# Loading the first batch's q and k in runs of eight rows per partition instead of four

## The chip, the cores and the metric

The kernel runs on one core of one Trainium2 chip. The metric is the device time of one execution in microseconds. Every kernel is run several times, beside the kernel before on the same chip. In the profile lines PE is TensorE, DVE VectorE, ACT ScalarE and POOL GpSimd. SBUF is the on-chip memory that the tiles stand in, PSUM the one that TensorE's results stand in.

## The reference

```python
def _attn_ref(q, k, v, tau):                      # B, N, C = 4, 6016, 256
    qn = q / (np.linalg.norm(q, axis=1, keepdims=True) + 1e-06)
    kn = k / (np.linalg.norm(k, axis=1, keepdims=True) + 1e-06)
    s = kn.transpose(0, 2, 1) @ qn / tau
    s = s - s.max(-1, keepdims=True)
    a = np.exp(s)
    a /= a.sum(-1, keepdims=True) + 1e-09
    return v @ a

def _moe_ref(x, w_gate, w_val, w_out):            # x: the 24064 x 256 rows of the above
    gate = 1.0 / (1.0 + np.exp(-(x @ w_gate)))
    return (gate * (x @ w_val)) @ w_out           # d_ff = 1536
```

The norms run over the 6016 rows, so one batch's scores, norms and 256 x 256 attention matrix need all of that batch's q and k before anything can be done with v. For batches 1 to 3 this is hidden behind the feed-forward of the batch before. For batch 0 nothing hides it.

## The kernel before

A partition holds 47 consecutive rows of a batch. Groups are four rows per partition (0 to 10), then two rows (group 11), then one (group 12). Group 0 comes as fp32 over two other queues; all else is loaded and cast to bf16 by DMAs that GpSimd issues, in one queue, in this order: q and k of groups 1 to 12, the first v, the expert weights (gate and value, in three column parts), the second v, the output weights.

```python
    def load_qk(b, t0, nt):
        tiles = []
        for name, src in (("q", q), ("k", k)):
            tl = qkpool.tile([P, TPC, C], BF16, tag=name, name=name + "_sb")
            nc.gpsimd.dma_start(out=tl[:, :nt, :], in_=rows(src, b)[:, t0 : t0 + nt, :])
            tiles.append(tl)
        qk[b, t0] = tiles
```

The work on batch 0, group by group: VectorE squares q, ScalarE squares k, VectorE adds both squares to bf16 accumulators, and TensorE adds the group to the scores. Small filler matmuls (`busy`) are meant to keep TensorE's clock up towards the end.

```python
    for g, (t0, nt) in enumerate(groups0):
        engines = (nc.vector, nc.scalar) if g < last0 else (nc.scalar, nc.vector)
        sq = [squares(0, t0, nt, w, engines[w], acc[w] if g == 0 else None) for w in range(2)]
        while adds:
            w, last_sq = adds.pop()
            nc.vector.tensor_tensor(out=acc[w], in0=acc[w], in1=last_sq, op=ALU.add)
        if 0 < g < n_acc:
            nc.vector.tensor_tensor(out=acc[0], in0=acc[0], in1=sq[0], op=ALU.add)
            if g < n_acc - 1:
                nc.vector.tensor_tensor(out=acc[1], in0=acc[1], in1=sq[1], op=ALU.add)
            else:
                adds.append((1, sq[1]))
        elif g:
            ends.append((sq, nt))
        if g == last0:
            norm_mms(ps_n0, acc, TPC, True, False)
            for n, (end, rows_n) in enumerate(ends):
                norm_mms(ps_n0, end, rows_n, False, n == len(ends) - 1, (1, 0) if n else (0, 1))
        for u in range(nt):
            score(0, t0, u)
        if n_acc - 4 <= g < n_acc:
            busy(1)
```

Then come the roots, the eps add (the 1e-6 of the reference is added to the norms) and the reciprocal, the scaled scores, the exponent, and the attention matrix folded into the expert weights (`ps_gh`); from there on TensorE runs to the end.

```python
    def norms_sqrt(b):
        s = st[b]
        s["r"] = attp.tile([P, 2 * CB], FP32, tag="r", name="r")
        nc.scalar.activation(out=s["r"], in_=s["n"], func=ACT.Sqrt)

    def norms_inv(b):
        r = st[b]["r"]
        nc.vector.tensor_scalar(out=r, in0=r, scalar1=1e-6, scalar2=None, op0=ALU.add)
        nc.vector.reciprocal(r, r)
```

## Time and profile before

| | before |
|---|---|
| time, median | 829.5 us |
| TensorE busy | 97% of the span |
| start to the first folded weight matmul (ps_gh) | 36.55 us |
| from there to the end | 791 us, TensorE without a break of note |
| DMA, 8 to 28 us | never idle, 209 GB/s written as bf16 |

The chain of waits reads from top to bottom as what had to end for the next piece to start. Its first 36 us are DMA, the rest is TensorE; so the kernel is bound by the bytes of batch 0 first and by TensorE afterwards, and only the first part can be touched by a change of loads. The prediction shows the lines.

### The profile page before, as it was taken

To read this page: it belongs to the slowest core of one execution; us is meant where nothing else is said; L and a number is where in the kernel's file an instruction comes from. 1 tells how busy PE (TensorE), PEld (TensorE's weight loads), DVE (VectorE), ACT (ScalarE), POOL (GpSimd) and SP (SyncE) were. 2 spreads that over 40 slices of the span, in tenths; PEclk is the share of its full clock that TensorE was granted. 3 is DMA by queue.
4 is the path that set the end of the run, shared out by engine and by line. 5 is a ranking of instruction groups with operands and counts; after the bars stand their busy time and mean duration, and the time that the engine had idled before them with its cause. 6 is when DMAs were issued, how large, how long until landed. Compare 5 with 4: busy or idle time off the path is not lost.

```text
span 827.7 us, 13626 instructions
## 1 busy us (share of the span) xinstructions
PE 806.9 (97%) x5122; PEld 498.5 (60%) x5134; DVE 591.5 (71%) x1027; ACT 390.8 (47%) x642; POOL 83.1 (10%) x159
## 2 busy tenths in 40 slices
PE   4799999999999999999999999999999999999998
PEld 2456666665665666665575666666566566666666
DVE  6777877787667777778767777777766666666665
ACT  4554444446644444445654444444655444444442
POOL 5532100002210100000311010000000000000000
PEclk9899999999999999999999999999999999999999
DMA  9999623226746443223876452223322323322211
GB/s 210 206 201 216 110 52 90 60 53 136 158 88 119 96 89 61 54 52 85 158 138 124 80 107 60 51 63 75 64 61 63 73 52 85 60 58 69 47 36 71
DMA packets 79026, 77.17 MB, mean 93 GB/s; under 512 B 50800, under 2 KB 55920, under 8 KB 78960
## 3 DMA queue, kind: packets, MB, share of 16 engines
q0 software_dynamic: 23920, 38.81, 28.1%
q1 hardware_dynamic: 54752, 36.91, 17.4%
q8 instruction: 40, 0.66, 0.3%
q10 hardware_dynamic: 288, 0.59, 0.2%
q14 instruction: 26, 0.21, 0.1%
HBM read 78.64 MB, written 24.64 MB: 125 GB/s over the span
## 4 chain that ended last, share of the span: by engine, by line
PE 94%; DMA 4%; DVE 1%; issue 0%; ACT 0%; POOL 0%; POOLq 0%
PE ps_o L88 30%; PE ps_gate L88 29%; PE ps_val L88 29%; PE ps_s L88 4%; DMA k_sb<-in_k_dram 3%; PE ps_gh L88 2%; DMA w_gate<-in_moe_w_gate_dram 1%; DVE hT L426 0%; ACT g_sb L425 0%; PE ps_end L88 0%; DVE sq L176 0%; PE ps_n L88 0%; POOL q_sb L97 0%; PE ps_tp L396 0%; DVE end L467 0%
## 5 line engine op out<-in xcount | busy, mean ns | idle before, releaser
L426 DVE TENSOR_TENSOR hT<-ps_val,g_sb 128x512 bf16<-128x512 f32 (+1 forms) x576 | 390.8, 679 | 205.6 <-ACT g_sb L425 201.0
L425 ACT ACTIVATE g_sb<-ps_gate 128x512 bf16<-128x512 f32 (+1 forms) x576 | 338.2, 588 | 386.2 <-PE ps_gate L88 380.2
L88 PE MATMUL ps_val<-vT,gh_H 128*128 128x512 bf16 (+1 forms) x1152 | 337.6, 375 | 0.3
L88 PE MATMUL ps_gate<-vT,gh_G 128*128 128x512 bf16 (+1 forms) x1152 | 337.5, 375 | 0.2
L88 PE MATMUL ps_o<-w_out_sb,hT 128*128 128x256 bf16 x2244 | 324.9, 273 | 0.0
L88 PEld LDWEIGHTS <-hT 128*128 128x128 bf16 x2268 | 221.0, 98 | 124.6
L88 PEld LDWEIGHTS <-gh_H 128*128 128x128 bf16 x1152 | 112.7, 98 | 132.1 <-issue 1.4
L88 PEld LDWEIGHTS <-gh_G 128*128 128x128 bf16 x1152 | 112.4, 98 | 37.6 <-ACT gh_G L379 0.2
L106 POOL DMA_DIRECT2D v_sb<-in_v_dram x48 | 25.5, 531 | 620.2 <-DMA vT<-v_sb 480.4
L452 DVE COPY out_sb<-ps_o 128x256 f32<-128x256 f32 x187 | 77.2, 413 | 12.6 <-PE ps_o L88 12.6
L88 PE MATMUL ps_s<-k_sb,q_sb 128*128 128x256 bf16 x376 | 70.5, 289 | 15.8 <-DMA k_sb<-in_k_dram 8.8
L88 PEld LDWEIGHTS <-q_sb 128*128 128x128 bf16 x376 | 38.6, 103 | 24.6 <-issue 9.6
L215 DVE TENSOR_TENSOR acc<-acc,sq 128x1024 bf16<-128x1024 bf16 (+1 forms) x66 | 44.1, 669 | 0.0
L176 DVE TENSOR_TENSOR sq<-q_sb 128x1024 bf16<-128x1024 bf16 (+2 forms) x44 | 29.3, 667 | 0.0
L97 POOL DMA_DIRECT2D q_sb<-in_q_dram x48 | 26.5, 552 | 15.2 <-DMA q_sb<-in_q_dram 7.3
L97 POOL DMA_DIRECT2D k_sb<-in_k_dram x48 | 26.2, 545 | 16.1 <-DMA k_sb<-in_k_dram 6.6
L176 DVE TENSOR_TENSOR sq<-k_sb 128x1024 bf16<-128x1024 bf16 (+2 forms) x34 | 22.4, 658 | 0.2 <-DMA k_sb<-in_k_dram 0.2
L174 ACT ACTIVATE sq<-k_sb 128x1024 bf16<-128x1024 bf16 (+1 forms) x11 | 11.2, 1019 | 13.6 <-DMA k_sb<-in_k_dram 13.6
L88 PE MATMUL ps_gh<-w_val,e_sb 128*128 128x512 bf16 x45 | 13.5, 379 | 0.2
L88 PEld LDWEIGHTS <-e_sb 128*128 128x128 bf16 x112 | 10.2, 98 | 5.3 <-DMA w_gate<-in_moe_w_gate_dram 0.6
L88 PE MATMUL ps_gh<-w_gate,e_sb 128*128 128x512 bf16 x41 | 12.7, 379 | 0.7 <-DMA w_gate<-in_moe_w_gate_dram 0.5
L425 ACT ACT_TABLE_LOAD x6 | 7.7, 1283 | 9.0 <-PE ps_gate L88 9.0
(69 smaller groups left out, 121.1 us busy)
## 6 DMA issues: line engine op xcount, KB each, us to landing
out_dram<-out_sb SPq DMA_DIRECT2D x44, 512.0 KB, 2.9
v_sb<-in_v_dram POOLq DMA_DIRECT2D x44, 256.0 KB, 3.8
q_sb<-in_q_dram POOLq DMA_DIRECT2D x43, 256.0 KB, 7.4
k_sb<-in_k_dram POOLq DMA_DIRECT2D x43, 256.0 KB, 8.1
out_dram<-out_sb SPq DMA_DIRECT2D x3, 384.0 KB, 3.1
w_gate<-in_moe_w_gate_dram POOLq DMA_DIRECT2D x3, 256.0 KB, 8.0
w_val<-in_moe_w_val_dram POOLq DMA_DIRECT2D x3, 256.0 KB, 8.1
w_out_sb<-in_moe_w_out_dram POOLq DMA_DIRECT2D x1, 768.0 KB, 13.3
```

The source lines that it names most:

```text
L88: nc.tensor.matmul(out, lhsT=lhsT, rhs=rhs, start=start, stop=stop, **kw)
L97: nc.gpsimd.dma_start(out=tl[:, :nt, :], in_=rows(src, b)[:, t0 : t0 + nt, :])
L106: nc.gpsimd.dma_start(out=v_sb[:, :nt, :], in_=rows(v, b)[:, t0 : t0 + nt, :])
L174: nc.scalar.activation(out=sq[:, :nt, :], in_=src[:, :nt, :], func=ACT.Square)
L176: engine.tensor_tensor(out=sq[:, :nt, :], in0=src[:, :nt, :], in1=src[:, :nt, :], op=ALU.mult)
L215: nc.vector.tensor_tensor(out=acc[:, :nt, :], in0=acc[:, :nt, :], in1=st[b]["sq", w][:, :nt, :], op=ALU.add)
L425: nc.scalar.activation(out=g_sb[:, :n], in_=ps_gate[:, :n], func=ACT.Sigmoid)
L426: nc.vector.tensor_tensor(out=hts[b, ci][:, f, :n], in0=ps_val[:, :n], in1=g_sb[:, :n], op=ALU.mult)
L452: nc.vector.tensor_copy(out=out_sb[:, s, :], in_=ps)
```

## The change

The intent: fewer and longer runs per partition for batch 0, so that the DMA queue has less overhead per byte. Groups 1 to 8 are loaded two at a time (eight rows, 8 KB read and 4 KB written per partition); groups 9 to 12 and all later batches keep their sizes. To hold eight rows the buffers are twice as large and there are 8 of them, not 12.

```diff
-    qkpool = pool("qkpool", NCH)
+    qkpool = pool("qkpool", 8)
...
-            tl = qkpool.tile([P, TPC, C], BF16, tag=name, name=name + "_sb")
+            tl = qkpool.tile([P, 2 * TPC, C], BF16, tag=name, name=name + "_sb")
             nc.gpsimd.dma_start(out=tl[:, :nt, :], in_=rows(src, b)[:, t0 : t0 + nt, :])
             tiles.append(tl)
-        qk[b, t0] = tiles
+        for u in range(0, nt, TPC):
+            qk[b, t0 + u] = [tl[:, u : u + TPC, :] for tl in tiles]
...
-    load_qk(0, *groups0[1])
+    pairs = [(t, 2 * TPC) for t in range(TPC, head - 3 * TPC, 2 * TPC)]
+    loads0 = pairs + [(t, n) for t, n in groups0 if t >= pairs[-1][0] + 2 * TPC]
+    load_qk(0, *loads0[0])
...
-    for t0, nt in groups0[2:]:
+    for t0, nt in loads0[1:]:
         load_qk(0, t0, nt)
```

## The prediction

> **What bounds the kernel now.** I read the page first (engine shares, the forty slices), then the chain of work that ended last from the start to 62 us, then the DMA rate between 9 and 27 us, and last the timeline between 22 and 38 us, engine by engine. The page says where to look:
>
> ```profile
> PE 94%; DMA 4%; DVE 1%; issue 0%; ACT 0%; POOL 0%; POOLq 0%
> ```
>
> From about 37 us to the end TensorE is the chain, and nothing in this change touches its instructions. The 4% of DMA is the only part that a different load of q and k can shorten. The chain in order of time shows it as one block at the head:
>
> ```profile
> 1.89 6.29 DMA k_sb<-in_k_dram
> ...
> 8.46 9.74 DMA k_sb<-in_k_dram
> ...
> 18.48 9.74 DMA k_sb<-in_k_dram
> ...
> 28.51 8.00 DMA w_gate<-in_moe_w_gate_dram
> ...
> 36.55 0.60 PE ps_gh L88 x2
> ```
>
> The columns are start, length and what. The loads of the first batch are back to back, and behind them in the same queue the first expert weights land at 36.51 us; TensorE starts the folded weights (ps_gh) then. This is a stretch set by bytes, not by latency: an issue is 9.74 us ahead of its landing only because about eight loads of 1.25 us each are queued. The DMA queue between 9 and 27 us:
>
> ```profile
> DMA packets 2066, 3.77 MB, mean 209 GB/s; under 512 B 227, under 2 KB 227, under 8 KB 2066
> q0 software_dynamic: 2066, 3.77, 112.1%
> ```
>
> 209 GB/s is of the bf16 written; twice that, 418 GB/s, is read as fp32. The engines are never idle here. The 2066 packets are 1839 data packets (2 KB written, 4 KB read) and 227 completion writes, so a run of four rows is one packet.
>
> Now the race at the end of the stretch, in the timeline (start, length, engine, line, operation, and the idle time before it with its releaser):
>
> ```profile
> 25.78 1.06 ACT L174 ACTIVATE sq<-k_sb 128x1024 bf16<-128x1024 bf16 x1 [1.43 <-DMA k_sb<-in_k_dram]
> 26.87 0.69 DVE L493 TENSOR_TENSOR acc<-acc,sq 128x1024 bf16<-128x1024 bf16 x1 [0.47 <-ACT sq L174]
> 27.48 0.68 DVE L176 TENSOR_TENSOR sq<-q_sb 128x1024 bf16<-128x1024 bf16 x1
> 28.20 0.69 DVE L491 TENSOR_TENSOR acc<-acc,sq 128x1024 bf16<-128x1024 bf16 x1
> 28.31 1.06 ACT L174 ACTIVATE sq<-k_sb 128x1024 bf16<-128x1024 bf16 x1 [1.47 <-DMA k_sb<-in_k_dram]
> 29.40 0.69 DVE L493 TENSOR_TENSOR acc<-acc,sq 128x1024 bf16<-128x1024 bf16 x1 [0.51 <-ACT sq L174]
> ...
> 31.88 0.69 DVE L489 TENSOR_TENSOR acc<-acc,sq 128x1024 bf16<-128x1024 bf16 x1
> ...
> 32.73 0.29 DVE L176 TENSOR_TENSOR sq<-k_sb 128x256 bf16<-128x256 bf16 x1 [0.16 <-DMA k_sb<-in_k_dram]
> ...
> 35.85 0.20 PE L88 MATMUL ps_r<-ones_bf,e_sb 128*128 128x1 bf16 x2 [0.35 <-ACT e_sb L316]
> ...
> 36.55 0.60 PE L88 MATMUL ps_gh<-w_gate,e_sb 128*128 128x512 bf16 x2 [0.49 <-DMA w_gate<-in_moe_w_gate_dram]
> ```
>
> Three things are to be seen. ScalarE starts a k square as each load lands, every 2.5 us. VectorE does three steps per group (square of q, add of q, add of k), spaced 0.61, 0.72 and 0.67 us when nothing holds it: 2.0 us in every 2.5, so it has 0.5 us of rest per group. And TensorE reached ps_gh 0.49 us before the weight landed, so the softmax branch (norms, exponent) has only half a microsecond of slack against the weight branch.
>
> **What the Trainium skill says.**
> 1. "DMA: Bandwidth & Descriptors", section "Where 436 GB/s comes from": the fabric gives 435 GB/s. The trace agrees that little is left: 418 GB/s, 96% of it. At the ceiling 1.049 MB (q and k of four rows) would take an estimated 2.41 us, not 2.51.
> 2. The same page, "Why small descriptors are slow (HBM only)": a fixed overhead of about 3 cycles per packet beside one cycle per 32 bytes. Estimate from it: 4096 bytes read are 128 + 3 cycles, 8192 are 256 + 3, so 1.2% less time per byte. No trace here has an 8 KB packet yet.
> 3. The same page, "Queues, rings and completion order": an engine alternates between its queues at packet granularity. Longer packets in the software queue can thus take share from the two fp32 loads of the first group, which ride another queue and took 4.8 and 5.0 us to land.
> 4. "TensorE: Matmul & The Clock Gate", "What's actually happening": an idle window of about 3.4 us brings half clock, a busy one brings it back. The trace agrees in kind: the same eight score matmuls took 1.03 us at 15.71 and 1.86 us at 18.24, after bursts with 1.5 us of idle.
>
> **The change, part by part.**
> - Removed: the first batch's groups 1 to 8 (rows 4 to 35) were 16 loads; they become 8 loads of twice the size. That is 8 x 128 = 1024 data packets and 8 x 16 = 128 completions fewer; the software queue should fall from 23,920 packets to 22,768, if a run of eight rows stays one packet. Bytes are the same.
> - DMA gain. 16 loads take 8 x 2.51 = 20.1 us. By the skill's 1.2%: 0.23 us. If the whole gap to 435 GB/s (0.10 us per pair of loads) is per packet and halves: 8 x 0.05 = 0.40 us. I take 0.3 us, on the landing of the last eight-row load and of everything behind it, the weights too (36.5 to about 36.2).
> - POOL issue: 8 issues of 0.53 us fewer; none was on the path, as POOL waited about 0.7 us for queue room before each. Worth 0.
> - Granularity, the cost. Group 7 (rows 28 to 31) used to land at 23.27; now it lands with group 8 at 25.76 (less the 0.3). VectorE therefore stands at 26.87 with the k add of group 7, where before it was at the k add of group 8: it is one group, 2.0 us, behind, and from there it has no rest. Walk it with the spacings above: k add 7 at 26.87; square, add, add of 8 at 27.48, 28.20, 28.87; of 9 at 29.48, 30.20, 30.87; square and add of q of 10 at 31.48 and 32.20; the two-row square at 32.87; the last k add at 33.36 instead of 31.88; the one-row square after 33.95 instead of 32.73. ScalarE is never late here (two squares of 1.06 us from 25.78, group 9 at 28.31). The norm matmuls end at about 34.6 instead of 33.35, 1.27 us later.
> - On the path: of the 1.27 us the first 0.49 are slack, so 0.78 remains. With the DMA gain both branches move 0.3 earlier, and the softmax branch is now the later one: 0.78 - 0.3 = +0.48 us.
> - Buffers: 8 of eight rows in place of 12 of four. Later batches take one per four-row group, a group every 8 slots of the schedule, loaded 20 slots ahead and used for about 8: four to five live at once. Eight are enough; worth 0. The one load of the first batch that reuses a buffer waits for group 0, whose last use is near 10 us.
> - After the start: about 790 us of TensorE chain, unchanged.
>
> Sum: 829.5 + 0.5 = 830.0 us.
>
> **The rivals.**
> (a) Long runs read better than the packet estimate, and VectorE catches up sooner. For it: someone chose to leave the last three groups short, which is what one does to keep the tail of the landing fine. Against: only 4% is left to the ceiling, 0.8 us over 20 us. It would make 828.7 to 829.3.
> (b) An eight-row run is cut into two packets, or its cast goes slower. Then only the backlog is left: +0.8, 830.3; slower packets by 5% would add 1 us. Nothing in the profile shows a packet over 4 KB read.
> (c) TensorE's clock. Score work now comes in 16 matmuls every 5 us with nearly 3 us of idle, so more of it runs at half clock; but 16 slow ones take 3.7 us, below 5, and with the filler matmuls from 25.8 on it is busy nearly without a break, so it should be at full clock by 30. If it were slow in the folded weights, up to 1.7 us would be added: 831.7.
> (d) Eight buffers hold up later loads. It would show as POOL waiting and TensorE idling after 100 us; TensorE is at 9 tenths in every slice now. I give it 3%.
> (e) The first fp32 group lands up to 0.5 us later (point 3). VectorE has 0.5 us rest per group before group 7, so it is absorbed: 0.
>
> **Range and chances.** The terms are -0.2 to -0.8 (DMA) and 0 to +0.8 (backlog), with (c) as a tail upward. Predicted 829.9, a touch below the sum because (a) is likelier than (b); 8 in 10 between 828.7 and 831.2. Two per cent is 16.6 us, more than half of the whole stretch that is touched: faster 0.01, same 0.98, slower 0.01.
>
> **What would show it.** The rate between 9 and 25 us: 421 to 425 GB/s read (210.5 to 212.5 in the page's count); 1152 packets fewer. ScalarE's k squares in twos, 5 us apart. VectorE without idle from about 26.6 to 33.6, and the one-row square near 33.7, not 32.7. Before ps_gh no wait for the weight load any more, but a longer one of ps_r for the exponent. TensorE's ps_gh from about 37.0. It is wrong if VectorE rests again before the last group, if ps_gh starts before 36.3, or if the time after 40 us grows by itself.

## The result and the profile after

The changed kernel took 830.08 us (median of 6 runs, 829.94 to 830.38) against 829.50 us (829.35 to 829.66, 6 runs). The ratio is 1.0007, with a 95% interval of 0.9994 to 1.0020: the same within 2%. Run once more later, it took 830.36 us against 829.71 us (ratio 1.0011). The interval includes 1. Still, in both rounds the slowest run of the kernel before (829.66, then 829.76) is faster than the fastest of the changed one (829.94, then 830.25); what the half microsecond is made of is read from the traces below.

The page of the changed kernel, packets of the software queue and the chain by engine:

```profile
q0 software_dynamic: 22768, 38.81, 28.3%
...
PE 94%; DMA 2%; DVE 2%; POOL 1%; ACT 0%; issue 0%; POOLq 0%; ACTq 0%
```

The packets fell by exactly the 1152 predicted, so an eight-row run stayed one packet. DMA lost half of its share of the chain (4% to 2%); VectorE (1% to 2%) and GpSimd (0% to 1%, its issues at the very start) took it over. The queue between 9 and 25 us of the changed kernel:

```profile
DMA packets 963, 3.40 MB, mean 212 GB/s; under 512 B 112, under 2 KB 112, under 8 KB 963
```

In the same window the kernel before moved 209 GB/s. Now the chain in order of time of the changed kernel (start, length, what), first 45 us:

```profile
6.26 18.92 DMA k_sb<-in_k_dram
...
25.26 1.07 ACT sq L180
26.35 0.69 DVE acc L499
27.05 0.61 DVE sq L182
27.68 0.69 DVE acc L497
...
32.57 0.61 DVE acc L495
...
33.23 0.67 PE ps_n L88 x20
...
34.12 0.74 DVE r L288
...
37.12 0.45 PE ps_gh L88 x2
```

Before, the chain went from loads to the weight load and into ps_gh. Now it leaves the DMA at 25.22 us, when the fourth eight-row k has landed, and goes through VectorE without a gap to the norms at 33 us. That is the backlog the prediction described. (The chain shows ps_gh at 37.12 us, where the ps_r matmuls before it end; it started at 36.98.) One line is odd: the eps add on `r`, four numbers per partition, lasts 0.74 us. The timeline around it, all engines, changed kernel:

```profile
33.09 0.28 DVE L182 TENSOR_TENSOR sq<-k_sb 128x256 bf16<-128x256 bf16 x1
...
33.80 1.06 POOL L150 DMA_DIRECT2D w_out_sb<-in_moe_w_out_dram  x1
...
34.12 0.73 DVE L288 TENSOR_SCALAR r<-r 128x4 f32<-128x4 f32 x1 [0.75 <-ACT r L284]
...
36.92 0.20 PE L88 MATMUL ps_r<-ones_bf,e_sb 128*128 128x1 bf16 x2 [0.36 <-ACT e_sb L322]
36.98 0.59 PE L88 MATMUL ps_gh<-w_gate,e_sb 128*128 128x512 bf16 x2
```

The same two lines of the kernel before:

```profile
33.08 0.73 POOL L139 DMA_DIRECT2D w_val<-in_moe_w_val_dram  x1
...
33.59 0.21 DVE L282 TENSOR_SCALAR r<-r 128x4 f32<-128x4 f32 x1 [0.56 <-ACT r L278]
```

In both kernels the eps add ends within 0.01 us of the end of a DMA issue on GpSimd (34.12 + 0.73 = 34.85 against 33.80 + 1.06 = 34.86; 33.59 + 0.21 = 33.80 against 33.08 + 0.73 = 33.81). Before, it started near the end of an issue; now it starts early in the long issue of the output weights. The Trainium skill, "SBUF — State Buffer", section "Who interferes with whom", offers a reason: VectorE and GpSimd share one pair of SBUF ports, `tensor_scalar` can enter a mode that needs both pairs, and whichever of the two starts first holds the pair for its whole instruction. Two of the experiments test this.

Everything after the start is moved as one block. Before, the second set of v transposes on TensorE starts at 50.04 us and the last matmul group (ps_end) at 822.96; after, at 50.47 and 823.39. Both differences are 0.43 us, which is also the difference of ps_gh (36.98 - 36.55). The medians differ by more, 0.58 us: the trace of the kernel before is of a run at 829.76 us, 0.26 above its median, and that of the changed kernel of one at 830.02, near its own.

### The profile page after: what moved, and what is told of

Same layout as the page of the kernel before. It is cut to its first block, busy times and chain, and to the rows that moved or that the text cites. A ratio compares the mean times of both kernels' runs of the same rounds, so it can differ in the third digit from the quotient of the medians.

```text
span 828.1 us, 13627 instructions
## 1 busy us (share of the span) xinstructions
PE 808.6 (98%) x5134; PEld 498.9 (60%) x5134; DVE 591.7 (71%) x1027; ACT 390.4 (47%) x642; POOL 78.8 (10%) x151
## 4 chain that ended last, share of the span: by engine, by line
PE 94%; DMA 2%; DVE 2%; POOL 1%; ACT 0%; issue 0%; POOLq 0%; ACTq 0%
PE ps_o L88 30%; PE ps_val L88 29%; PE ps_gate L88 29%; PE ps_s L88 4%; PE ps_gh L88 2%; DMA k_sb<-in_k_dram 2%; DVE sq L182 0%; DVE hT L432 0%; POOL q_sb L98 0%; DVE acc L497 0%; DVE acc L499 0%; ACT g_sb L431 0%; PE ps_n L88 0%; POOL k_sb L98 0%; PE ps_end L88 0%
## 5 line engine op out<-in xcount | busy, mean ns | idle before, releaser
L98 POOL DMA_DIRECT2D q_sb<-in_q_dram x44 | 24.1, 548 | 40.5 <-PE ps_s L88 14.6
L98 POOL DMA_DIRECT2D k_sb<-in_k_dram x44 | 24.0, 545 | 14.0 <-DMA k_sb<-in_k_dram 7.7
```

## The experiments

**Theory.** Three terms act in the first 37 us, and what they sum to is carried unchanged to the end: the longer runs bring the data earlier; the fourth eight-row load leaves VectorE a group behind with no rest left to catch up; and the eps add then falls into GpSimd's issue of the output weights. **Rivals:** the smaller pool of larger buffers costs the time; long runs cost time wherever they stand; the long eps add is something else than a port held by GpSimd.

All of these results were correct, and all times are medians of five runs (nine of the kernel before, in the same rounds).

### Buffers alone

```diff
-    loads0 = pairs + [...]                 # four-row loads, buffers as in the change
+    loads0 = groups0[1:]
```

> Eight buffers of eight rows as in the change, but every load four rows, as before. Theory (the change acts only in the first 37 us, by fewer and longer runs and by later group 7): 829.5 us like the kernel before, within 0.15; 23,920 packets in the software queue, score groups 2.51 us apart, folded weights (ps_gh) from about 36.5 us with a wait on the weight load. Rival (the smaller pool of larger buffers costs the time, by later loads or by addresses): 830.0 us, with ps_gh still at 36.5 and the time lost after 40 us.

829.40 us against 829.49 (ratio 0.9999, interval 0.9987 to 1.0012). ps_gh started at 36.27 us behind the weight load, and the time from the second transposes to ps_end was 772.92 us, as in the kernel before. The buffers cost nothing that shows; that rival falls. The loads are those of the kernel before, so the 0.28 us between the two traces at ps_gh is the spread from run to run: the first weights landed at 36.2 us here, at 36.5 there.

### The eps add reads PSUM

```diff
-        nc.scalar.activation(out=s["r"], in_=s["n"], func=ACT.Sqrt)
+        nc.scalar.activation(out=s["n"], in_=s["n"], func=ACT.Sqrt)
...
-        nc.vector.tensor_scalar(out=r, in0=r, scalar1=1e-6, ...)
+        nc.vector.tensor_scalar(out=r, in0=st[b]["n"], scalar1=1e-6, ...)
```

> The changed kernel, but the square roots of the norms stay in PSUM and VectorE's eps add reads them there, so that it has no SBUF source. Theory (the eps add took 0.73 us in the changed kernel because GpSimd held the shared SBUF ports while it wrote the descriptors of the output weight load): it takes 0.15 to 0.25 us, ps_gh starts about 0.5 us sooner, at 36.4 to 36.5, and the time is 829.5 us. Rival (the 0.73 us is something else, such as a late semaphore, or nothing that is on the path): the eps add or the step after it stays long and the time is 830.0 us.

829.63 us against 829.49 (ratio 1.0002, interval 0.9990 to 1.0015). The timeline of this kernel:

```profile
33.96 1.06 POOL L150 DMA_DIRECT2D w_out_sb<-in_moe_w_out_dram  x1
34.26 0.16 DVE L288 TENSOR_SCALAR r<-ps_n 128x4 f32<-128x4 f32 x1 [0.74 <-ACT ps_n L284]
34.46 0.18 DVE L289 RECIPROCAL r<-r 128x4 f32<-128x4 f32 x1
...
36.54 0.59 PE L88 MATMUL ps_gh<-w_gate,e_sb 128*128 128x512 bf16 x2
```

The same issue is under way and the add runs through it in 0.16 us. From the start of the add to ps_gh it now takes 2.28 us; in the changed kernel it was 2.86. So about 0.57 us of the add (0.73 - 0.16) was waiting. The reciprocal right after it reads and writes SBUF inside the same issue and takes 0.18 us, as in the kernel before: a source in SBUF alone does not make a VectorE instruction wait.

### The output weights are issued first

```diff
-    load_v(0, 1)
     nc.gpsimd.dma_start(out=w_out_sb, in_=moe_w_out.rearrange("(t p) c -> p t c", p=P))
+    load_v(0, 1)
```

> The changed kernel with GpSimd's issue of the output weight load (1.06 us) put ahead of the issue of the second v load (0.58 us). Theory (port lock): the output weight issue runs from about 33.3 to 34.3 us, the eps add can start at 34.1 and ends within 0.02 us of that issue's end, so it lasts about 0.2 us unless the v issue takes the port first, in which case it lasts until 34.85 again; ps_gh at about 36.45, 829.5 us. Rival (the 0.73 us belongs to VectorE or the semaphore, not to GpSimd): it stays 0.73 us whatever GpSimd does, 830.0 us.

830.15 us against 829.72 (ratio 1.0005, interval 0.9992 to 1.0017). The median did not fall to 829.5 as expected, and no run shows why; the trace is of the fastest of the five runs (829.80). In it the step under test did what the theory says:

```profile
33.51 1.05 POOL L149 DMA_DIRECT2D w_out_sb<-in_moe_w_out_dram  x1
34.37 0.20 DVE L288 TENSOR_SCALAR r<-r 128x4 f32<-128x4 f32 x1 [0.75 <-ACT r L284]
34.52 0.60 POOL L108 DMA_DIRECT2D v_sb<-in_v_dram  x1
...
36.68 0.59 PE L88 MATMUL ps_gh<-w_gate,e_sb 128*128 128x512 bf16 x2
```

The add starts later in the issue and ends again with it (34.57 against 34.56), so it lasts only 0.20 us. It ends with the issue in two other runs too, where it came early in it: 0.73 us with one end at 35.15 and the issue's at 35.16 (last pair only, below), and 0.64 us with 35.00 and 35.01 (three pairs, below). With the run above this settles that GpSimd's issue sets the end of this add when its source lies in SBUF. That the ports are the reason is the skill's explanation; the PSUM run and the reciprocal fit it and no run contradicts it.

### The last pair only

```diff
-    loads0 = pairs + [...]
+    loads0 = groups0[1:7] + [(7 * TPC, 2 * TPC)] + groups0[9:]
```

> Only groups 7 and 8 (rows 28 to 35) in one eight-row load, the rest in four-row loads. Theory: the whole backlog with only a quarter of the DMA gain (0.1 us), so the k of group 8 lands near 25.6 us, VectorE has no idle time from there on, the norm matmuls end near 34.2 us, the eps add is held until the output weight issue ends (about 35.2 us) or runs free if it falls after it, ps_gh starts at 37.2 to 37.5 us and the time is 830.3 us. Rival (the loss is not the backlog): 829.5 us.

830.59 us against 829.49 (ratio 1.0016, interval 1.0004 to 1.0029). The lines of ScalarE and VectorE:

```profile
25.57 2.00 ACT L179 ACTIVATE sq<-k_sb 128x1024 bf16<-128x1024 bf16 x2 [3.88 <-DMA k_sb<-in_k_dram]
26.66 0.69 DVE L498 TENSOR_TENSOR acc<-acc,sq 128x1024 bf16<-128x1024 bf16 x1 [2.22 <-ACT sq L179]
...
33.39 0.28 DVE L181 TENSOR_TENSOR sq<-k_sb 128x256 bf16<-128x256 bf16 x1
```

No other VectorE line between 26.66 and 33.39 has an idle time: one long load is enough for the whole backlog. ps_gh started at 37.27 us, 0.29 later than in the changed kernel, which is what three of the four long loads had gained there. So the last long load alone is enough for the harm, backlog and held add together (ps_gh is 0.72 us later than in the kernel before). The median is 0.3 above the expectation; two of the five runs were at 831.5 and 831.7 us, with no trace.

### A twelve-row load last

```diff
-            tl = qkpool.tile([P, 2 * TPC, C], BF16, tag=name, name=name + "_sb")
+            if nt > 2 * TPC:
+                tl = attp.tile([P, nt, C], BF16, tag="long" + name, name=name + "_sb")
+            else:
+                tl = qkpool.tile([P, 2 * TPC, C], BF16, tag=name, name=name + "_sb")
...
+    loads0 = [(4, 8), (12, 8), (20, 4), (24, 12)] + groups0[9:]
```

> The double dose: the last long load takes twelve rows (24 to 35), so VectorE is two groups behind where it was one. Theory: the k of groups 6, 7 and 8 lands together near 25.3 us, VectorE has no idle time from there to the end, the norm matmuls end 1.9 us later than in the changed kernel, at 35.8; the eps add falls after the output weight issue and takes 0.2 us; ps_gh at 38.3 us and 831.4 us. Rival (the backlog does not set the end): 830.0 us or less, since the runs are longer still.

832.71 us against 829.71 (ratio 1.0031, interval 1.0017 to 1.0045). The timeline, ScalarE, VectorE and TensorE:

```profile
25.56 3.90 ACT L182 ACTIVATE sq<-k_sb 128x1024 bf16<-128x1024 bf16 x4 [6.20 <-DMA k_sb<-in_k_dram]
26.64 0.69 DVE L501 TENSOR_TENSOR acc<-acc,sq 128x1024 bf16<-128x1024 bf16 x1 [3.35 <-ACT sq L182]
...
35.31 0.28 DVE L184 TENSOR_TENSOR sq<-k_sb 128x256 bf16<-128x256 bf16 x1
...
35.66 0.44 PE L88 MATMUL ps_n<-ones_bf,sq 128*128 128x1 bf16 x12
...
36.34 0.17 DVE L290 TENSOR_SCALAR r<-r 128x4 f32<-128x4 f32 x1 [0.75 <-ACT r L286]
```

Twelve rows at once leave VectorE another group behind. From its first add after the landing to the one-row square it takes 8.67 us (35.31 - 26.64); in the changed kernel it was 6.74 (33.09 - 26.35). The difference, 1.93 us, is one group of VectorE work, as expected. The eps add fell after all issues and lasted 0.17 us. The time is 1.3 us above the expectation because of something it had left out: TensorE had nothing to do for 5.24 us before the landing and later waited for the norms, and its clock was down when they came (0.54 from 36.2 to 39.4 us, 1.00 in the changed kernel). The fp32 matmuls of ps_rk took 1.06 us, not 0.68, and ps_gh began at 39.38 us instead of 38.3. The trace is of a run at 832.82; two of the five runs took 831.65 and 831.76, near the expectation, and were not traced.

### Four long loads, VectorE relieved

```diff
-        if 0 < g < n_acc:
+        if 0 < g < n_acc and g != 8:          # no adds for group 8 on VectorE
...
-        elif g:
+        elif g and g != 8:
...
-            norm_mms(ps_n0, acc, TPC, True, False)
+            norm_mms(ps_n0, acc, TPC, False, False)
...
+        if g == 8:
+            norm_mms(ps_n0, sq, nt, True, False)   # TensorE sums group 8's squares
```

> The changed kernel, all four eight-row loads kept, but the squares of group 8 go straight to TensorE (16 one-column matmuls) and VectorE's two adds for that group, 1.3 us, are dropped. Theory (VectorE's backlog behind the fourth eight-row load is what put the norms late, not the loads themselves): VectorE rests again before the one-row square, the norm matmuls end near 33.0 us, 0.9 sooner than the 33.9 of the changed kernel; the eps add then meets GpSimd's issue of the last weight or of v and may lose 0.1 to 0.5 us; ps_gh starts behind the weight load at 36.0 to 36.2 and the undisturbed run takes 829.1 to 829.3 us. Rival (the loss sits in the long loads themselves): 830.0 us.

829.89 us against 829.71 (ratio 1.0003, interval 0.9991 to 1.0016). The loads are those of the change, but VectorE rests again (the last square waits for its load), and ps_gh starts 1.28 us sooner than in the changed kernel:

```profile
32.31 0.29 DVE L182 TENSOR_TENSOR sq<-k_sb 128x256 bf16<-128x256 bf16 x1 [0.15 <-DMA k_sb<-in_k_dram]
...
33.21 0.18 DVE L288 TENSOR_SCALAR r<-r 128x4 f32<-128x4 f32 x1 [0.60 <-ACT r L284]
...
35.70 0.60 PE L88 MATMUL ps_gh<-w_gate,e_sb 128*128 128x512 bf16 x2
```

So the long loads themselves are not what cost the time. Some 0.3 of the 1.28 us needed luck as well: the first weights landed at 35.6 us here, at 36.0 in the changed kernel, and ps_gh cannot start before them. Three of the fourteen traces have them by 35.7, the other eight with long loads between 35.9 and 36.4; no run says why. The gain did not arrive in full, for two reasons. The second set of transposes started at 49.52 us, 0.95 sooner and not 1.28, because TensorE now waited for the next weight parts: the DMA had become the limit again. And in this one trace 0.54 us were lost later: from those transposes to ps_end it took 773.46 us, where 10 of the 14 traces have 772.92 or 772.93. I have no explanation for that.

### Three pairs

```diff
-    pairs = [(t, 2 * TPC) for t in range(TPC, head - 3 * TPC, 2 * TPC)]
+    pairs = [(t, 2 * TPC) for t in range(TPC, head - 5 * TPC, 2 * TPC)]
```

> The changed kernel with three eight-row loads instead of four (rows 4 to 27); groups 7 to 10 are four-row loads. Theory (the last eight-row load leaves VectorE one group behind, and it needs three or four groups to make that up): VectorE rests again before group 10, the norm matmuls end near 33.0 us, the DMA gain is 0.3 to 0.45 us, ps_gh starts at about 36.1 us with a wait on the weight load, and the time is 829.1 us. Rival (eight-row loads cost time wherever they stand): between 829.7 and 830.0 us.

830.32 us against 829.49 (ratio 1.0006, interval 0.9993 to 1.0020); four runs at 830.2 to 830.4, one at 829.32. The expectation failed. The backlog did go: the one-row square came at 32.34 us, as early as in the relieved kernel. But TensorE was late:

```profile
27.84 1.03 PE L88 MATMUL ps_s<-k_sb,q_sb 128*128 128x256 bf16 x8 [1.24 <-DMA k_sb<-in_k_dram]
...
30.37 1.74 PE L88 MATMUL ps_s<-k_sb,q_sb 128*128 128x256 bf16 x8 [1.29 <-DMA k_sb<-in_k_dram]
...
33.65 0.46 PE L88 MATMUL ps_n<-ones_bf,sq 128*128 128x1 bf16 x12
```

The eight matmuls at 30.37 took 1.74 us, those at 27.84 took 1.03. The stretches say why: from 30.4 to 33.8 us the granted clock was 0.52 here and 1.00 in the kernel before. The norm matmuls ended at 34.11 us for it, 0.8 later than in the kernel before, and the eps add then fell into the output weight issue (0.64 us), so ps_gh came at 37.12.

### Three pairs, roots in PSUM

This is the three-pair kernel with the edit of "The eps add reads PSUM".

> Three eight-row loads and the norms' roots in PSUM, so neither the backlog nor the port wait is left. The three-pair kernel alone showed TensorE at half clock from 30 to 33 us and a port wait of 0.64 us. Theory (clock and port were what hid its gain): where TensorE keeps full clock ps_gh starts at about 36.1 us behind the weight load and the run takes 829.1 us; where it drops, the norms come 0.8 us later, and ps_gh starts near 36.5: 829.5 us. Rival (shorter runs at the end do not help at all): 830.0 us and more.

829.99 us against 829.72 (ratio 1.0002, interval 0.9990 to 1.0015); runs from 829.25 to 830.43. The trace is of the 829.25 run: full clock, eps add 0.16 us, one-row square at 32.50, ps_gh at 36.24 behind the weight load. In this run theory and trace agree, but it is the fastest of five, and the others were not traced. Its loads are those of the three-pair trace, where the clock fell.

### The same with more fillers, and the kernel before with both edits

```diff
-            busy(1)
+            busy(3 if g < n_acc - 1 else 1)
```

> Three eight-row loads, roots in PSUM, and three filler matmuls instead of one after each of groups 7, 8 and 9. Theory (a drop of TensorE's clock between groups made the three-pair runs uneven): the clock stays full from 27 us on, the norm matmuls end near 33.0 us, ps_gh starts at 36.0 to 36.2 us, set by the weight load, and all runs lie within 0.3 us of 829.1 us, faster than both kernels. Rival (the fillers delay the scores): ps_gh after 36.5 and 829.5 us or more.

830.23 us against 829.72 (ratio 1.0010, interval 0.9996 to 1.0023); 829.28, 830.06, 830.23, 830.58 and 831.13. In the trace, of the 829.28 run, the eight score matmuls took 1.03 us in every four-row group from 23 us on, and ps_gh began at 35.82, with the first weights early (35.7). The expectation that all runs would lie near 829.1 failed.

> The kernel before (four-row loads throughout) with the roots in PSUM and the same three fillers. Theory (there the weight load's landing at 36.5 us is the limit, and norms and clock have slack): 829.5 us, as before, perhaps without its single run at 830.3. Rival (the gain of the other kernel comes from fillers and PSUM, not from longer runs): 829.1 us, as that one.

830.28 us against 829.72 (ratio 1.0007, interval 0.9995 to 1.0020), with runs from 829.32 to 831.36: neither theory nor rival. Its trace, of a run at 830.31, shows a late landing:

```profile
34.04 0.29 DVE L176 TENSOR_TENSOR sq<-k_sb 128x256 bf16<-128x256 bf16 x1 [1.56 <-DMA k_sb<-in_k_dram]
```

The one-row k landed at about 34.0 us, where 32.7 is usual, and the norms waited for it. This kernel has only four-row loads, so late landings do not need long runs. It also means that the two edits may cost time by themselves (0.56 us in the median here), so the medians of the other kernels that carry them do not show the worth of the loads alone.

### Relieved and roots in PSUM

> The relieved kernel with the roots of the norms in PSUM as well. Theory: neither backlog nor port wait is left, the eps add takes 0.16 us, ps_gh starts behind the weight load at 36.0 to 36.2 us, 829.1 us in undisturbed runs and the median below that of the kernel before by 0.3. Rival (the uneven runs seen in the three-pair kernels belong to eight-row loads and eat the gain): fastest run at 829.1 to 829.3 but a median of 829.7 or more, with runs above 830.3.

829.89 us against 829.71 (ratio 1.0007, interval 0.9995 to 1.0020); 829.62 to 831.20. The rival's wording fits the median and the spread, but not the fastest run, which it put at 829.1 to 829.3. The trace has the late landing too: the one-row square waited 1.40 us for its load and came at 33.68, and ps_gh came at 36.79. No kernel of this study is faster than the kernel before in its median beyond the noise (buffers alone by 0.09 us), so there is no better version to offer.

### The changed kernel again

> The changed kernel once more, to stand beside the others on the same chip. Theory: 830.0 us, 0.5 to 0.6 above the kernel before, eps add again about 0.73 us and ended by the end of the output weight issue. Rival (part of the difference is the chip or the day): 829.5 to 829.7 us.

830.36 us against 829.71, four runs at 830.25 to 830.52 and one at 831.39. The eps add took 0.74 us and ended at 35.00, with the output weight issue; ps_gh at 37.12. The mechanism of the first trace repeats.

### All starts side by side

Times in us, each from one trace, whose run took the time in the column "traced run"; the last column is the median of all runs minus that of the kernel before in the same rounds.

| kernel | one-row square | eps add | ps_gh | second transposes | ps_end | traced run | median difference |
|---|---|---|---|---|---|---|---|
| before | 32.73 | 0.21 | 36.55 | 50.04 | 822.96 | 829.76 | 0 |
| buffers alone | 32.56 | 0.17 | 36.27 | 49.81 | 822.73 | 829.38 | -0.09 |
| changed | 33.09 | 0.73 | 36.98 | 50.47 | 823.39 | 830.02 | +0.58 |
| changed, again | 33.22 | 0.74 | 37.12 | 50.60 | 823.72 | 830.52 | +0.65 |
| eps from PSUM | 33.24 | 0.16 | 36.54 | 50.02 | 822.95 | 829.60 | +0.14 |
| output weights first | 33.33 | 0.20 | 36.68 | 50.17 | 823.18 | 829.80 | +0.43 |
| last pair only | 33.39 | 0.73 | 37.27 | 50.75 | 823.67 | 830.46 | +1.10 |
| twelve rows last | 35.31 | 0.17 | 39.38 | 53.16 | 826.08 | 832.82 | +3.00 |
| relieved | 32.31 | 0.18 | 35.70 | 49.52 | 822.98 | 829.70 | +0.18 |
| relieved, PSUM | 33.68 | 0.16 | 36.79 | 50.28 | 823.13 | 829.62 | +0.18 |
| three pairs | 32.34 | 0.64 | 37.12 | 50.60 | 823.52 | 830.15 | +0.83 |
| three pairs, PSUM | 32.50 | 0.16 | 36.24 | 49.73 | 822.65 | 829.25 | +0.27 |
| three pairs, PSUM, fillers | 32.70 | 0.16 | 35.82 | 49.66 | 822.58 | 829.28 | +0.51 |
| before, PSUM, fillers | 34.04 | 0.16 | 37.16 | 50.64 | 823.57 | 830.31 | +0.56 |

In ten of these rows ps_end is 772.92 or 772.93 us after the second transposes (772.92 = 822.96 - 50.04); three more are within 0.2 us of it, and the relieved kernel lost 0.54. The start decides; the rest is carried along.

## Why the prediction was right

- **What bounds the kernel, and where a change can act.** Right. The difference of 0.43 us stands at ps_gh and is still 0.43 at the end.
- **DMA gain.** Right, in size too. ScalarE's squares begin as the k loads land. From the second group's k to the eighth's they are 15.08 us apart before (10.70 to 25.78) and 15.09 and 15.11 in the two other kernels with four-row loads alone; with the change they are 14.77 (10.49 to 25.26), and 14.76 to 14.82 in the five other traces with its loads. So three eight-row loads of q and k gained 0.31 us, 0.10 each. The first one shows no gain: the second group's k landed at 10.63 us on average in these six traces and at 10.60 in the three with four-row loads, so the eighth group's k came 0.29 us sooner (25.41 against 25.70), the 0.3 that was taken. What in a load was saved, packets or completion writes, is not shown; both fell. The reading "whole gap to 435 GB/s" has no support from the page that the prediction cites: that figure is the ceiling of the SBUF ports, where 209 GB/s of bf16 arrive, and the same section puts the limit of a read from HBM (the chip's main memory) at about 358 GB/s, which the 418 measured here, with one core running, exceed; the measurement decides. That half of the gap agrees with the measured gain per load is no proof of it.
- **Backlog.** The step is right: VectorE has no idle time from 26.35 to 33.09 us. It was mis-sized. The walk put the one-row square at 33.95, less 0.3 for the DMA; it came at 33.09. The k add follows the q add after 0.61 us when nothing holds it, not after 0.67 (which was read where a square follows the q add), so a group takes 1.93 us, and the half-size steps at the end follow each other more closely too (33.09 - 31.54 = 1.55 from the last full q add, where the walk had 1.75). The norm matmuls ended at 33.88 us, where the prediction implies 34.3.
- **What it left out.** The eps add's collision with GpSimd's issue, 0.53 us (0.73 against 0.21). So the sum was right because two errors cancel, and that is luck: the norms came about 0.4 us earlier than predicted, and the step after them took 0.5 us longer. With the eps add in PSUM, ps_gh is back at 36.54 us and the median is 0.14 us above the kernel before: backlog and DMA gain alone make about +0.1, not +0.5, as far as the spread of 0.3 us between traces lets one say.
- **Slack.** The 0.49 us of slack of the softmax branch is used up: no wait for the weight load is left before ps_gh. The sign that was named, a longer wait of ps_r for the exponent, did not show (0.36 against 0.35), because TensorE was itself late: it waited for the last k add and for the reciprocal.
- **Buffers and issue.** Zero, as predicted; the first experiment shows it for the buffers.
- **The first fp32 group.** Rival (e) fits, and it cost nothing that shows. In the first pair of traces nothing is to be seen (VectorE's cast began at 5.46 us, before at 5.59), but the trace before is the odd one: ScalarE's cast of k began at 5.43, 5.43, 5.50 and, in that trace, 5.79 us where the first loads have four rows, and at 5.66 to 5.96 in the ten with eight. That the longer packets are the reason is not shown.
- **TensorE's clock.** For the changed kernel it was at full speed from 30 us on, as predicted. The rival was underrated all the same: it hid the gain of the three-pair kernel and made the twelve-row kernel 1 us slower than its backlog.

## What to carry to other kernels

A longer transfer gives its gain per byte to the queue and its cost to whoever waits for the whole of it: before making transfers longer, compare the idle time of the busiest consumer per group with the work that will now arrive at once, and end the stretch early enough for it to be worked off. When a step moves by half a microsecond, look at what it now stands beside; a four-element instruction became 0.5 us longer only because another engine's DMA issue was under way. And a sum that comes out right does not prove its terms: read each of them in the trace.

## What stays open

Late landings of the small last loads (about 1 us) were seen in two traces, and single runs of 831.1 to 831.7 us in four of the altered kernels (and 831.39 in the repeat of the changed one), besides the twelve-row kernel, while the kernel before had none above 830.4 in 33 runs. One of the four has only four-row loads, so long runs are not needed for it; what the cause is, no run here tells. The 0.54 us lost late in the relieved kernel's trace is open too.

## What the Trainium skill lacked or had wrong

- "DMA: Bandwidth & Descriptors", "Why small descriptors are slow (HBM only)": the three cycles per packet stated there give 1.2% less time per byte for 8 KB reads than for 4 KB reads (an estimate from the page); with the 32 bytes of descriptor metadata that it also names, taken as one more cycle, 1.5% (also an estimate). The traces show 2.1%: 14.78 us on average of six against 15.09 of three for the same bytes. The page has no figure for the completion writes, which also fell (128 fewer); no run separates them.
- "SBUF — State Buffer", "Who interferes with whom": the rule agrees with the traces. What the page lacks is the size for GpSimd writing descriptors first: an add of 128 x 4 fp32 in SBUF lasted up to 0.74 us where it takes 0.17 with no issue under way and 0.16 from PSUM, and it ended within 0.01 us of the end of the DMA issue in all eight traces in which it started inside one. bf16 adds of two SBUF tiles kept their 0.69 us beside such issues, as the page infers.
- "TensorE: Matmul & The Clock Gate", "What's actually happening": the page's table ties the drop to an idle window of about 3.4 us; a later section names frequent short idle times as well, but gives no busy share. In the three-pair kernel no gap after 25 us was longer than 1.29 us and the clock still fell to 0.52 from 30.4 us. TensorE was busy for 1.27 us of the 3.4 us before that; in the kernel before, and in the three-pair kernel with the roots in PSUM, it was busy for 1.25 us of the same stretch and the clock stayed at 1.00. So a stretch that is a little over a third busy lost the clock in one trace and kept it in two.
